# An attention gradient kernel: 32-row operands, steps in a fixed order, and some transposed probabilities from DMA instead of a second exponential

## The chip, the core and the metric

The kernel runs on one core of a Trainium2 chip. The metric is device time in microseconds (us) of one execution. TensorE multiplies matrices and writes to PSUM, ScalarE (ACT in the profile) does the exponentials, VectorE (DVE) and GpSimd (POOL) do element-wise work, and the DMA queues move and transpose data. Each kernel was timed in alternation with the kernel before on the same chip.

## The reference, cut to what matters

The reference is forward and backward of `out = x + attention(xn) * silu(mlp(xn))`, with 2048 positions, width 512, 32 heads of 16 channels, and gradients for x and all weights. The attention part is this; the change touches nothing else.

```python
scores = jnp.einsum("bhqd,bhkd->bhqk", q, k) * (Dh ** -0.5)   # 32 heads, 2048 x 2048
p = softmax(scores)
o = jnp.einsum("bhqk,bhkd->bhqd", p, v)                       # and, by jax.vjp, dq, dk, dv
```

## The kernel before

Two heads (a pair) are worked on together. The attention stage has 64 blocks (16 pairs times 4 groups of 512 queries) of 16 steps. In step g of a block (cut, names as in the kernel):

```python
# keys on partitions, 128 keys x 2 heads x 512 queries, for block j
s  = K^T Q        # TensorE     et = exp(s)     # ScalarE
d  = V^T dO       # TensorE     gts = d * et    # VectorE;  gk = transpose of gts by DMA
X += [V,K | 1 | ...] * et, gts   # TensorE: sums over keys, give o, row sums L and dq
# queries on partitions, for block j-1, whose row sums are known by now
t  = Q^T K        # TensorE     e = exp(t)      # ScalarE: the same probabilities a second time, transposed
Z += W1 * e + W2 * gk            # TensorE: sums over queries, give dk and dv; added to acc by VectorE
```

At the end of a block, X is copied (`xs`), transposed on TensorE (`XT`), copied (`xt`), and a chain of small operations on VectorE (`rL`, `dl`, `ndr`) and GpSimd makes `W1` and `W2` for the Z products. The parts that the change touches:

```python
ps_s = ... bufs=1        # s: one buffer, [128, 2, 512] fp32
ps_d = ... bufs=2        # t and d take turns in two buffers of the same size
def emit_r1(g):          # s(g), t(g), d(g), in this order
    ...
    for hj in range(2):
        r0 = 64 * hj     # each head takes 64 array rows; a pair fills all 128
        nc.tensor.matmul(s[:, hj, :], lhsT=op["KVT"][r0:r0 + 64, ...], rhs=op["QT"][r0:r0 + 64, ...], tile_position=(r0, 0))
    ...                  # t and d likewise
for g in range(...):     # the framework's scheduler may still move these
    emit_r1(g + 1)       # so d(g+1) is asked for before the multiply of step g
    emit_exp_a(g); emit_mult(g); emit_exp_b(g); emit_dmat(g)
    ...                  # X products of step g-1, Z products of step g-3
```

Of the kernel before, what the change touches and what calls it, by code (L numbers as in the profile page):

```python
# [8 lines left out]
bf16 = mybir.dt.bfloat16  # L9
# [533 lines left out]
NATW_CORE = 33  # L543
def attention_core(ctx, tc, NAT_s, NATQ_s, Oall, dQall, dKVT_out,
                   ident_f32, npairs=16, lagb=3, nqc=4, ekc=(), laga=1):
    nc = tc.nc
    S = 2048
    opnd = ctx.enter_context(tc.tile_pool(name="opnd", bufs=1))
    ps_s = ctx.enter_context(tc.tile_pool(name="ps_s", bufs=1, space=PSUM))
    ps_x = ctx.enter_context(tc.tile_pool(name="ps_x", bufs=1, space=PSUM))  # L550
    ps_z = ctx.enter_context(tc.tile_pool(name="ps_z", bufs=1, space=PSUM))
    ps_d = ctx.enter_context(tc.tile_pool(name="ps_dt", bufs=2, space=PSUM))
    ps_t = ps_d
    etp = ctx.enter_context(tc.tile_pool(name="etp", bufs=3 + laga))
    gtp = ctx.enter_context(tc.tile_pool(name="gtp", bufs=5))
    etsp = ctx.enter_context(tc.tile_pool(name="etsp", bufs=3)) if ekc else None
    gbp = ctx.enter_context(tc.tile_pool(name="gbp", bufs=6))
    ekp = ctx.enter_context(tc.tile_pool(name="ekp", bufs=2)) if ekc else None
    ep = ctx.enter_context(tc.tile_pool(name="ep", bufs=lagb + 2))
    xsp = ctx.enter_context(tc.tile_pool(name="xsp", bufs=1))  # L560
    finp = ctx.enter_context(tc.tile_pool(name="finp", bufs=2))
    wp = ctx.enter_context(tc.tile_pool(name="wp", bufs=2))
    accp = ctx.enter_context(tc.tile_pool(name="accp", bufs=1))
    outp = ctx.enter_context(tc.tile_pool(name="outp", bufs=1))

    OP = []
    for i in range(2):
        t = dict(
            KVT=opnd.tile([128, S], bf16, name=f"KVT{i}"),
            QT=opnd.tile([128, S], bf16, name=f"QT{i}"),  # L570
            DOT=opnd.tile([128, S], bf16, name=f"DOT{i}"),
            NAT=opnd.tile([128, 16, 2, NATW], bf16, name=f"NAT{i}"),
            NATQq=opnd.tile([128, 16, 2, 17], bf16, name=f"NATQq{i}"),
            NATQd=opnd.tile([128, 16, 2, 16], bf16, name=f"NATQd{i}"),
        )
        OP.append(t)
    KPad = opnd.tile([128, 16, 2, 64], bf16, name="KPad")
    QPad = opnd.tile([128, 16, 2, 64], bf16, name="QPad")
    DPad = opnd.tile([128, 16, 2, 64], bf16, name="DPad")
    nc.gpsimd.memset(KPad[:], 0.0)  # L580
    nc.gpsimd.memset(QPad[:], 0.0)
    nc.gpsimd.memset(DPad[:], 0.0)
# [3 lines left out]
    cur_op = {}  # L586
    load_q = []

    def load_pair(p, immediate=False):
        t = OP[p % 2]  # L590
        cur_op[p] = t
        eng = nc.sync
        ops = []

        def plain():
            eng.dma_start(out=t["NAT"][:].rearrange("q k j c -> q k (j c)"), in_=NAT_s[p])
            eng.dma_start(out=t["NATQq"][:].rearrange("q k j c -> q k (j c)"), in_=NATQ_s[0][p])
            eng.dma_start(out=t["NATQd"][:].rearrange("q k j c -> q k (j c)"), in_=NATQ_s[1][p])
        ops.append(plain)

        def tk():
            nc.gpsimd.tensor_copy(out=KPad[:, :, :, 0:NATW], in_=t["NAT"][:])
            eng.dma_start_transpose(out=t["KVT"][:].rearrange("r (m k) -> r m k", m=16), in_=KPad[:].rearrange("q k j c -> q (k j c)"))
        ops.append(tk)

        def tq():
            nc.gpsimd.tensor_copy(out=QPad[:, :, :, 0:17], in_=t["NATQq"][:])
            eng.dma_start_transpose(out=t["QT"][:].rearrange("r (m k) -> r m k", m=16), in_=QPad[:].rearrange("q k j c -> q (k j c)"))
        ops.append(tq)

        def td():
            nc.gpsimd.tensor_copy(out=DPad[:, :, :, 17:33], in_=t["NATQd"][:])
            eng.dma_start_transpose(out=t["DOT"][:].rearrange("r (m k) -> r m k", m=16), in_=DPad[:].rearrange("q k j c -> q (k j c)"))
        ops.append(td)
        if immediate:
            for o in ops:
                o()
        else:
            load_q.extend(ops)
# [4 lines left out]

    st_s = {}; st_d = {}; st_t = {}; st_et = {}; st_e = {}; st_gt = {}; st_ets = {}
    blk = [dict() for _ in range(NB + 1)]
    cur = dict(Z=None, gts=None)

    def a_unit(g):
        j = g // 16  # L630
        return (j, g % 16) if j < NB else None
# [4 lines left out]

    def emit_r1(g):
        a = a_unit(g); b = b_unit(g)
        if a is not None:
            j, kb = a  # L640
            p, qc = blocks[j]
            op = cur_op[p]
            s = ps_s.tile([128, 2, 512], f32, name="s")
            st_s[g] = s
            for hj in range(2):
                r0 = 64 * hj
                nc.tensor.matmul(s[:, hj, :], lhsT=op["KVT"][r0:r0 + 64, kb * 128:(kb + 1) * 128],  # L647
                                 rhs=op["QT"][r0:r0 + 64, qc * 512:(qc + 1) * 512],
                                 start=True, stop=True, tile_position=(r0, 0))
        if b is not None and b[1] not in ekc:  # L650
            j, kc, qb = b
            p, qc = blocks[j]
            op = cur_op[p]
            t = ps_t.tile([128, 2, 512], f32, name="t", tag="d")
            st_t[g] = t
            q0 = (qc * 4 + qb) * 128
            for hj in range(2):
                r0 = 64 * hj
                nc.tensor.matmul(t[:, hj, :], lhsT=op["QT"][r0:r0 + 64, q0:q0 + 128],  # L659
                                 rhs=op["KVT"][r0:r0 + 64, kc * 512:(kc + 1) * 512],  # L660
                                 start=True, stop=True, tile_position=(r0, 0))
        if a is not None:
            j, kb = a
            p, qc = blocks[j]
            op = cur_op[p]
            d = ps_d.tile([128, 2, 512], f32, name="d", tag="d")
            st_d[g] = d
            for hj in range(2):
                r0 = 64 * hj
                nc.tensor.matmul(d[:, hj, :], lhsT=op["KVT"][r0:r0 + 64, kb * 128:(kb + 1) * 128],  # L670
                                 rhs=op["DOT"][r0:r0 + 64, qc * 512:(qc + 1) * 512],
                                 start=True, stop=True, tile_position=(r0, 0))
        while fin_pending and fin_pending[0][1] <= g:
            emit_finalize(fin_pending.pop(0)[0])

    def emit_exp_a(g):
        a = a_unit(g)
        if a is None:
            return
        j, kb = a  # L680
        if (kb // 4) in ekc:
            if kb % 2 == 0:
                cur["ets"] = etsp.tile([128, 2, 2, 512], bf16, name="ets")
            ets = cur["ets"]
            st_ets[g] = ets
            et = ets[:, kb % 2]
        else:
            et = etp.tile([128, 2, 512], bf16, name="et")[:]
        st_et[g] = et
        nc.scalar.activation(out=et, in_=st_s.pop(g)[:], func=ACT.Exp)  # L690

    def emit_mult(g):
# [3 lines left out]
        j, kb = a  # L696
# [4 lines left out]
        nc.vector.tensor_tensor(out=gts[:, kb % 2], in0=st_d.pop(g)[:], in1=st_et[g], op=ALU.mult)  # L701

    def emit_dmat(g):
        a = a_unit(g)
        if a is None:
            return
        j, kb = a
        if kb % 2 == 1:
            kc = kb // 4
            kbp = (kb // 2) % 2  # L710
            if kbp == 0:
                blk[j].setdefault("Gk", {})[kc] = gbp.tile([128, 2, 16, 128], bf16, name="gk")
            gk = blk[j]["Gk"][kc]
            nc.sync.dma_start_transpose(out=gk[:, kbp], in_=st_gt[g][:].rearrange("k a h q -> k (a h q)"))
            if kc in ekc:
                if kbp == 0:
                    blk[j].setdefault("Ek", {})[kc] = ekp.tile([128, 2, 16, 128], bf16, name="ek")
                ek = blk[j]["Ek"][kc]
                nc.sync.dma_start_transpose(out=ek[:, kbp], in_=st_ets.pop(g)[:].rearrange("k a h q -> k (a h q)"))
                st_ets.pop(g - 1, None)  # L720

    def emit_exp_b(g):
        if b_unit(g) is None or b_unit(g)[1] in ekc:
            return
        e = ep.tile([128, 2, 512], bf16, name="e")
        st_e[g] = e
        nc.scalar.activation(out=e[:], in_=st_t.pop(g)[:], func=ACT.Exp)  # L727

    def emit_acc_a1(g):
        a = a_unit(g)  # L730
        if a is None:
            return
# [271 lines left out]
```

## Time and profile before

| | before |
|---|---|
| median time | 3006.6 us (3003.4 to 3009.0, 4 runs) |
| attention stage | 287 to 2393 us |
| median block | 32.66 us |
| exponentials per block | 32, one every 0.905 us at best: 29.0 us |

First the costliest groups on the page of the kernel before (line, engine, operation, out<-in, shapes, count | busy us, mean ns of one | idle time before them and what ended it).

```profile
L701 DVE TENSOR_TENSOR gts<-d,et 128x1024 bf16<-128x1024 f32 x1024 | 1251.5, 1222 | 555.9 <-ACT et L690 534.5
L690 ACT ACTIVATE et<-s 128x1024 bf16<-128x1024 f32 x1024 | 1050.5, 1026 | 161.5 <-PE s L647 126.7
L727 ACT ACTIVATE e<-t 128x1024 bf16<-128x1024 f32 x1024 | 1049.5, 1026 | 6.2 <-PE t L659 5.0
```

A mean of 1026 ns is not what an exponential costs. In the view of the instructions of the kernel before in time order, from which the next lines are taken (start us, duration us, engine, line, operation, [idle before <- what ended it]), one ScalarE instruction starts before the one ahead of it has ended.

```profile
1193.04 1.02 ACT L727 ACTIVATE e<-t 128x1024 bf16<-128x1024 f32 x1
...
1193.17 1.23 DVE L701 TENSOR_TENSOR gts<-d,et 128x1024 bf16<-128x1024 f32 x1 [0.84 <-ACT et L690]
...
1193.94 1.03 ACT L690 ACTIVATE et<-s 128x1024 bf16<-128x1024 f32 x1
1194.11 0.39 PE L659 MATMUL t<-KVT_2216,QT_2217 64*128 64x512 bf16 x2 [0.24 <-ACT e L727]
...
1194.45 0.39 PE L670 MATMUL d<-DOT_2218,KVT_2216 64*128 64x512 bf16 x2
...
1194.84 1.04 ACT L727 ACTIVATE e<-t 128x1024 bf16<-128x1024 f32 x1
...
1195.22 0.38 PE L829 MATMUL Z<-gk,W_14113 128*32 128x512 bf16 x2
...
1195.54 0.39 PE L647 MATMUL s<-QT_2217,KVT_2216 64*128 64x512 bf16 x2
...
1195.97 1.02 ACT L690 ACTIVATE et<-s 128x1024 bf16<-128x1024 f32 x1
```

From 1193.04 to 1193.94 and on to 1194.84 the starts are 0.90 us apart, with nothing idle. The Trainium skill, "ScalarE: Activation LUTs", "What ACT_TABLE_LOAD costs", says that back-to-back activations overlap by about 93 ns; here it is about 0.12 us. The next `et` starts only at 1195.97, 1.13 us after the `e` ahead of it, because its `s` (L647) started at 1195.54, at the end of a long row of products. So the steps alternate between about 1.83 and 2.03 us. Also note d (L670): at 1194.45 it starts 0.05 us after the multiply (L701, 1193.17 + 1.23) has ended. Of the eight steps between 1299 and 1316 us, six do the same, within 0.06 us; over the trace from 400 to 2150 us it is 87% of the d products. These start 0.34 us after their t, the others 0.22.

The view of busy time by stretch, for one stretch of 260 us of the kernel before, shows how full the engines are. Its columns are the stretch, its length, the busy us (and instructions) of PE, PE's weight loads, DVE, ACT and POOL, the granted TensorE clock, the DMA share and GB/s.

```profile
1000.00:1260.00 260.00, 234.14 (x2074) 68.94 (x2069) 192.83 (x208) 240.89 (x256) 29.03 (x78) 1.00 0.82 148
```

The view of the waits of the kernel before, between 400 and 2150 us (who <- for whom: us in total, times, longest), names who waits on ScalarE's path:

```profile
PE t L659 <- ACT e L727: 104.5, 394, 0.5
ACT et L690 <- PE s L647: 104.2, 152, 2.6
```

TensorE waits for `e` to give its buffer to t, and what stands behind t comes late, s among it, for which ScalarE then waits.

### The profile page before, as it was taken

What the parts mean: (1) busy time and instruction counts of PE and PEld (TensorE: products, weight loads), DVE (VectorE), ACT (ScalarE), POOL (GpSimd) and SP (SyncE); (2) the same over time, 40 slices, a digit from 0 to 9 for tenths busy, and PEclk for the clock granted to TensorE, in tenths of its full rate; (3) what the DMA queues carried; (4) which work ended last, traced back from release to release, by engine and by line L of the source; (5) the groups of instructions that cost most, each with busy time, mean ns of one, the idle gap of its engine ahead of it and who ended that gap; (6) DMA issues with size and microseconds to landing.
All of it is one profiled execution on the core that took longest, in us unless ns stands there. A gap on an engine that the chain in (4) does not pass through costs nothing. (4 is left out here: it accounts for less than half of the span.)

```text
span 2997.4 us, 50127 instructions
## 1 busy us (share of the span) xinstructions
PE 2491.3 (83%) x19909; PEld 859.6 (29%) x19968; DVE 2011.0 (67%) x2422; ACT 2205.8 (74%) x2485; POOL 583.2 (19%) x944
## 2 busy tenths in 40 slices
PE   3786998898899899899988988998898865665967
PEld 2332222222222222222222222222222233332443
DVE  5764777777777777777777777777777637882044
ACT  2442899998899999999999989999999824441020
POOL 0334011101101110110111011011101026881024
PEclk8898999999999999999999999999999987887989
DMA  5436888869878886987888698788867563325431
GB/s 169 120 127 145 142 151 138 162 130 157 142 147 149 142 162 132 160 145 148 153 138 161 132 158 142 148 153 137 162 132 130 107 230 94 103 81 153 127 127 41
DMA packets 1324301, 417.62 MB, mean 139 GB/s; under 512 B 1247393, under 2 KB 1308194, under 8 KB 1324066
## 3 DMA queue, kind: packets, MB, share of 16 engines
q1 hardware_dynamic: 1250674, 360.80, 63.0%
q10 hardware_dynamic: 73392, 53.62, 5.8%
q8 instruction: 156, 2.56, 0.3%
q14 instruction: 79, 0.65, 0.1%
HBM read 65.41 MB, written 55.32 MB: 40 GB/s over the span
## 5 line engine op out<-in xcount | busy, mean ns | idle before, releaser
L701 DVE TENSOR_TENSOR gts<-d,et 128x1024 bf16<-128x1024 f32 x1024 | 1251.5, 1222 | 555.9 <-ACT et L690 534.5
L690 ACT ACTIVATE et<-s 128x1024 bf16<-128x1024 f32 x1024 | 1050.5, 1026 | 161.5 <-PE s L647 126.7
L727 ACT ACTIVATE e<-t 128x1024 bf16<-128x1024 f32 x1024 | 1049.5, 1026 | 6.2 <-PE t L659 5.0
L742 PE MATMUL X<-et,Lc 128*32 128x512 bf16 x2048 | 403.2, 389 | 2.3 <-DVE xt L776 0.2
L659 PE MATMUL t<-KVT_2216,QT_2217 64*128 64x512 bf16 x1024 | 200.5, 380 | 63.8 <-ACT e L727 61.4
L659 PE MATMUL t<-KVT_2222,QT_2223 64*128 64x512 bf16 x1024 | 200.1, 380 | 64.0 <-ACT e L727 61.3
L647 PE MATMUL s<-QT_2217,KVT_2216 64*128 64x512 bf16 x1024 | 201.3, 388 | 15.2 <-DMA QT_2217<-QPad 15.1
L670 PE MATMUL d<-DOT_2218,KVT_2216 64*128 64x512 bf16 x1024 | 201.0, 381 | 11.8 <-DVE gts L701 6.2
L670 PE MATMUL d<-DOT_2224,KVT_2222 64*128 64x512 bf16 x1024 | 200.4, 380 | 4.8 <-DVE gts L701 2.8
L647 PE MATMUL s<-QT_2223,KVT_2222 64*128 64x512 bf16 x1024 | 199.9, 387 | 0.0
L758 PE MATMUL X<-gts,NAT_2219 128*17 128x512 bf16 x1024 | 198.0, 381 | 0.0
L758 PE MATMUL X<-gts,NAT_2225 128*17 128x512 bf16 x1024 | 197.4, 381 | 0.0
L745 PE MATMUL X<-et,NAT_2219 128*32 128x512 bf16 x1024 | 196.8, 391 | 0.0
L745 PE MATMUL X<-et,NAT_2225 128*32 128x512 bf16 x1024 | 196.4, 390 | 0.0
L742 PEld LDWEIGHTS <-Lc 128*32 128x32 bf16 x2048 | 100.4, 93 | 245.1 <-issue 236.8
L659 PEld LDWEIGHTS <-QT_2223 64*128 64x128 bf16 x1024 | 89.2, 94 | 188.7 <-issue 188.5
L659 PEld LDWEIGHTS <-QT_2217 64*128 64x128 bf16 x1024 | 89.2, 94 | 185.8 <-issue 185.6
L837 DVE TENSOR_TENSOR acc<-Z,acc 64x512 f32<-64x512 f32 x192 | 129.3, 673 | 8.7 <-PE Z L829 8.7
L670 PEld LDWEIGHTS <-KVT_2216 64*128 64x128 bf16 x1024 | 90.0, 93 | 138.4 <-issue 127.9
L670 PEld LDWEIGHTS <-KVT_2222 64*128 64x128 bf16 x1024 | 90.6, 93 | 126.4 <-issue 118.6
L647 PEld LDWEIGHTS <-KVT_2216 64*128 64x128 bf16 x1024 | 52.1, 93 | 224.9 <-issue 223.7
L647 PEld LDWEIGHTS <-KVT_2222 64*128 64x128 bf16 x1024 | 49.1, 93 | 218.0 <-issue 218.0
(1527 smaller groups left out, 3829.7 us busy)
## 6 DMA issues: line engine op xcount, KB each, us to landing
gk<-gts SPq DMA_TRANSPOSE x512, 4.3
HG_s<-hg SPq DMA_DIRECT2D x16, 448.0 KB, 2.9
GB_s<-gB ACTq DMA_DIRECT2D x16, 256.0 KB, 2.0
dKVT_s<-ob SPq DMA_DIRECT2D x16, 256.0 KB, 3.6
dhc<-DH_s ACTq DMA_DIRECT2D x2, 2048.0 KB, 13.6
H1T_s<-h1row SPq DMA_DIRECT2D x14, 256.0 KB, 2.0
H1T_s<-h1row ACTq DMA_DIRECT2D x14, 256.0 KB, 2.0
h1T<-H1T_s SPq DMA_DIRECT2D x8, 448.0 KB, 3.8
```

The source lines that it names most:

```text
L647: nc.tensor.matmul(s[:, hj, :], lhsT=op["KVT"][r0:r0 + 64, kb * 128:(kb + 1) * 128], rhs=op["QT"][r0:r0 + 64, qc * 512:(qc + 1) * 512], st ...
L659: nc.tensor.matmul(t[:, hj, :], lhsT=op["QT"][r0:r0 + 64, q0:q0 + 128], rhs=op["KVT"][r0:r0 + 64, kc * 512:(kc + 1) * 512], start=True, st ...
L670: nc.tensor.matmul(d[:, hj, :], lhsT=op["KVT"][r0:r0 + 64, kb * 128:(kb + 1) * 128], rhs=op["DOT"][r0:r0 + 64, qc * 512:(qc + 1) * 512], s ...
L690: nc.scalar.activation(out=et, in_=st_s.pop(g)[:], func=ACT.Exp)
L701: nc.vector.tensor_tensor(out=gts[:, kb % 2], in0=st_d.pop(g)[:], in1=st_et[g], op=ALU.mult)
L727: nc.scalar.activation(out=e[:], in_=st_t.pop(g)[:], func=ACT.Exp)
L742: nc.tensor.matmul(X[64 + 32 * hj:64 + 32 * hj + 32, :], lhsT=Lc[:, :], rhs=et[:, hj, :], start=(kb == 0), stop=False, skip_group_check=Tr ...
L745: nc.tensor.matmul(X[32 * hj:32 * hj + 32, :], lhsT=NATt[:, kb, hj, 1:33], rhs=et[:, hj, :], start=(kb == 0), stop=(kb == 15), tile_positi ...
L758: nc.tensor.matmul(X[64 + 32 * hj:64 + 32 * hj + 17, :], lhsT=NATt[:, kb, hj, 0:17], rhs=gts[:, kb % 2, hj, :], start=False, stop=(kb == 1 ...
L837: nc.vector.tensor_tensor(out=av, in0=Z[0:64, :], in1=av, op=ALU.add)
```

## The change

The intent: s, t and d take 32 rows each, so that d can run beside s; the steps are put in a fixed order by hand (`tc.manual_schedule()`), with s and t in turn in two buffers and d in two of its own; and 2 of the 16 `e` tiles of a block are not computed again but are DMA transposes (`ek`) of `et`. I call these two units the DMA part. The diff, cut to its core:

```diff
-    ps_s = ... (name="ps_s", bufs=1, space=PSUM)     # [128, 2, 512]
-    ps_d = ... (name="ps_dt", bufs=2, space=PSUM)    # [128, 2, 512], t and d
+    dma_units = ((1, 3), (3, 3))                     # (key group kc, query block qb) without a second exp
+    ps_st = ... (name="ps_st", bufs=2, space=PSUM)   # [128, 2, 512], s and t
+    ps_d = ... (name="ps_d", bufs=2, space=PSUM)     # [128, 512], one head of d each; XT too
 ... KVT, QT, DOT become KVT and QDT: 32 rows each for K0, K1, V0, V1 and q0, q1, dO0, dO1
+    def emit_t(g):
+        if b is None or b[1:] in dma_units:
+            return
 ...
+            r = 64 + 32 * hj
+            d = ps_d.tile([128, 512], f32, name="d", tag="d")
+            nc.tensor.matmul(d[:], lhsT=op["KVT"][r:r + 32, ...], rhs=op["QDT"][r:r + 32, ...], ..., tile_position=(r, 0))
 ...
-        nc.vector.tensor_tensor(out=gts[:, kb % 2], in0=st_d.pop(g)[:], in1=st_et[g], op=ALU.mult)
+        for hj in range(2):
+            nc.vector.tensor_tensor(out=gts[:, kb % 2, hj, :]..., in0=ds[hj][:]..., in1=st_et[g][:, :, kb % 4, hj, :], op=ALU.mult)
 ...
+                if (kc, qb) in dma_units:
+                    ek = ekp.tile([128, 8, 128], bf16, name="ek")
+                    nc.sync.dma_start_transpose(out=ek[:], in_=st_et[g][:, qb].rearrange("k a h q -> k (a h q)"))
 ...
+        emit_t(g)
+        if not first:
+            emit_le(g - 1)          # X products of et
+        emit_exp_b(g)
+        emit_s(g + 1)
+        emit_d(g)
+        emit_mult(g)
+        emit_exp_a(g + 1)
+        emit_dmat(g)
+        if first:
+            emit_le(g - 1)
+        emit_g(g - 1)               # X products of gts
+        emit_z(g - lagb, 0)         # Z products of e or ek
+        emit_z(g - lagb, 1)         # Z products of gk
+        if g >= 17 and (g - 17) % 16 == 0 and (g - 17) // 16 < NB:
+            emit_finalize((g - 17) // 16)
```

The small copies for `dKVT` go to GpSimd, and the operand transposes fall from three to two per pair.

## The prediction

> **What bounds it now.** The attention stage runs from 287 to about 2395 us, 70% of the span (instructions in time order): 64 blocks of 16 steps, about 32.5 us a block. A step has two 1024-wide exponentials on ScalarE, `et<-s` and `e<-t`. The groups give 1026 ns each, but in the time order one starts 0.905 us after the other when nothing holds it: ends overlap. So ScalarE's floor is 1.81 us a step, 29.0 us a block. Normal steps alternate between 1.83 and 2.05 us (mean 1.94): `s` has one PSUM buffer, and TensorE, in order, does s, t, d, X and Z products (about 1.5 us of slots of 0.22 to 0.34 us) with waits for `e` in between, so `s` comes late at times (`et <- PE s` in the waits: 113 us between 400 and 2300). The end of a block (XT transposes, W1, W2) costs about 1.5 us more. VectorE is busy 74% of the stage, DMA 82%; a 512 KB `gk` transpose streams for 2.5 us of every 4.
>
> **What changes.**
> 1. Two of 16 `e` exponentials per block become DMA transposes of `et`: 2 x 0.905 us off ScalarE, floor 27.2 us a block.
> 2. s, t, d take 32 rows each; d sits in other rows than s and follows it, so all four should run together. The Trainium skill, "TensorE: Matmul & The Clock Gate", Part 3, says that small matmuls in different row groups run concurrently. The trace agrees for pairs of 64 rows (one slot of 0.22 us); four of 32 no trace here shows yet. TensorE goes from six slots a step to five, about 1.4 us.
> 3. `s` and `t` alternate in two buffers: `s` can run during the preceding `e`, `t` during the preceding `et`, each with about 0.4 us to spare. ScalarE should be gapless in normal steps.
> 4. The multiply is split in two 512-wide ones with a one-bank d each. From the 512-wide copies (0.68 us, ends overlapping by 0.08) I estimate 0.6 us each, 1.2 us a step against 1.14. With acc, xs, xt and small ones VectorE needs 23.5 to 25 us a block, near ScalarE's floor but below.
> 5. DMA: per pair 32 `gk` as before, plus 8 half-size `ek`, minus one of three operand transposes; streaming about 12.5 of every 14.5 us. Close, not binding.
> 6. Steps without `e` can't quite keep 0.905 us: TensorE brings `t` about 0.2 us late. At the end of a block XT in the d buffers holds up d and t: I keep 1.0 us.
>
> **Sum.** 14 x 1.83 + 2 x 1.05 + 1.0 = 28.7 us a block against 32.5, nearly all on the critical path, as ScalarE paces the stage. 63 blocks x 3.8 = 240 us, a little more in the first. Other stages don't change. I predict 2760 us, range 2690 to 2850; faster by over 2%: 0.96, within 2%: 0.03, slower: 0.01.
>
> **What would show it.** `e<-t` 896 times, still 1.03 us; ScalarE starts 0.905 us apart in normal steps, busy over 95% of the stage's middle; `et <- PE s` well under 113 us; s and d starting together; `gts` 2048 times near 0.68 us; DMA share about 0.95; block period 28 to 29.5 us.
>
> **What would make it wrong.** Strided 256-byte runs slow the exponential or the multiply; VectorE (d single-buffered per half) becomes the pace; in-order TensorE waits for d and passes that to t; DMA queueing delays `gk`; four-row matmuls don't overlap.

## The result, and the profile after

| | before | after |
|---|---|---|
| median time | 3006.6 us | 2848.6 us (2847.5 to 2850.9, 4 runs) |
| ratio | | 0.948 (0.946 to 0.949) |
| median block | 32.66 us | 30.44 us |

Ratios here are the mean time of one kernel's runs over that of the other's of the same rounds, so not quite the ratio of the medians. The gain is 158 us; I had predicted 247. It lies in the attention stage, as foreseen: `et` starts there at 287 us in both, and the last `e` ends at 2392.9 us before and 2253.9 after.

The same groups on the page of the kernel after:

```profile
L697 DVE TENSOR_TENSOR gts<-d,et 128x512 bf16<-128x512 f32 x2048 | 1315.0, 683 | 374.6 <-ACT et L676 146.4
L676 ACT ACTIVATE et<-s 128x1024 bf16<-128x1024 f32 x1024 | 1058.1, 1056 | 11.8 <-PE d L662 11.7
L684 ACT ACTIVATE e<-t 128x1024 bf16<-128x1024 f32 x896 | 933.9, 1043 | 165.0 <-PE t L634 163.9
```

The multiply is 683 ns, as estimated, and `et` no longer waits for s. But `e<-t` waits 163.9 us for t, where before `e` had almost no idle time. The waits of the kernel after in the same window say it again:

```profile
ACT e L684 <- PE t L634: 144.1, 233, 1.0
...
PE s L648 <- ACT et L676: 108.6, 458, 0.5
```

Now s waits for ScalarE instead of ScalarE for s; t is the one that comes late.

In the same stretch of the kernel after, the DMA share is 0.98 (predicted 0.95), and VectorE is up from 193 to 208 us of 260.

```profile
1000.00:1260.00 260.00, 237.49 (x2188) 72.94 (x2180) 208.49 (x349) 238.90 (x258) 33.72 (x88) 1.00 0.98 171
```

Where the waits sit becomes plain from the time between the starts of consecutive `et`, taken from each trace, as a median per position in the block over blocks 4 to 59 (us; position 0 is from the block's first `et` to its second):

```
position       0    1    2    3    4    5    6    7    8    9   10   11   12   13   14   15
before      2.06 1.82 2.67 1.82 3.00 1.82 2.03 1.83 2.07 1.82 2.03 1.83 2.06 1.82 2.03 1.83
after       2.82 1.81 2.66 1.81 2.19 1.81 1.81 0.90 2.79 1.81 1.81 1.81 1.88 1.81 1.81 0.90
```

Normal steps after are 1.81 us, gapless, as predicted. Positions 7 and 15 are the steps without `e`: 0.90 us, one exponential saved. But the steps right behind them, 8 and 0, take 2.8 us, one microsecond too much. What was saved is given back one step later. This is one such place in the kernel after (instructions in time order):

```profile
1182.57 0.39 PE L648 MATMUL s<-QDT,KVT 32*128 32x512 bf16 x2
...
1182.58 0.39 PE L662 MATMUL d<-QDT,KVT 32*128 32x512 bf16 x2
...
1183.09 1.29 DVE L697 TENSOR_TENSOR gts<-d,et 128x512 bf16<-128x512 f32 x2 [0.60 <-ACT et L676]
...
1183.33 1.94 ACT L676 ACTIVATE et<-s 128x1024 bf16<-128x1024 f32 x2
...
1183.66 0.39 PE L648 MATMUL s<-QDT,KVT 32*128 32x512 bf16 x2
...
1183.84 0.37 PE L662 MATMUL d<-QDT,KVT 32*128 32x512 bf16 x1
1184.30 0.67 DVE L818 COPY acc<-Z 64x512 f32<-64x512 f32 x1
1184.43 0.37 PE L662 MATMUL d<-QDT,KVT 32*128 32x512 bf16 x1 [0.23 <-DVE gts L697]
...
1184.74 0.39 PE L744 MATMUL X<-gts,NAT 128*17 128x512 bf16 x2
...
1185.02 0.39 PE L807 MATMUL Z<-e,W 128*32 128x512 bf16 x2
...
1185.24 0.39 PE L813 MATMUL Z<-gk,W 128*32 128x512 bf16 x2
...
1185.57 0.39 PE L634 MATMUL t<-KVT,QDT 32*128 32x512 bf16 x2
...
1186.06 1.02 ACT L684 ACTIVATE e<-t 128x1024 bf16<-128x1024 f32 x1 [0.79 <-PE t L634]
```

At 1182.57 and 1182.58, s and d start together: the packing works as the Trainium skill, "TensorE: Matmul & The Clock Gate", Part 3, says of small matmuls in different row groups. At 1183.33 ScalarE does two `et` in a row (x2), for there is no t in this step. The next t (L634) could have started when the first of these was done, about 1184.3. But TensorE takes its work in order, and ahead of t stand the second half of d, which waits 0.23 us for the multiply that began at 1183.09; the X product of gts (0.31 us later); the Z product (0.28 us later, because `acc` (L818, started at 1184.30) still reads the one Z buffer); the second Z product (0.22 us); then t (0.33 us). So t starts at 1185.57 and `e` at 1186.06 after 0.79 us of idle time. The trace has the same sequence at all 112 steps of this kind in blocks 4 to 59: in the middle 80% of them t starts 2.28 to 2.31 us after the first of the two `et`. The prediction had said that t comes 0.2 us late. It had named d's wait, passed on to t, as a risk, but not put it into the sum.

### The profile page after: what moved, and what is told of

It is laid out like the page before. It is cut to its first block, busy times and chain, and to the rows that moved or that the text cites. A ratio compares the mean times of both kernels' runs of the same rounds, so it can differ in the third digit from the quotient of the medians.

```text
span 2849.1 us, 50869 instructions
## 1 busy us (share of the span) xinstructions
PE 2397.8 (84%) x19712; PEld 845.8 (30%) x19712; DVE 2029.7 (71%) x3382; ACT 2057.1 (72%) x2357; POOL 619.0 (22%) x1023
## 5 line engine op out<-in xcount | busy, mean ns | idle before, releaser
L697 DVE TENSOR_TENSOR gts<-d,et 128x512 bf16<-128x512 f32 x2048 | 1315.0, 683 | 374.6 <-ACT et L676 146.4
L684 ACT ACTIVATE e<-t 128x1024 bf16<-128x1024 f32 x896 | 933.9, 1043 | 165.0 <-PE t L634 163.9
L662 PE MATMUL d<-QDT,KVT 32*128 32x512 bf16 x2048 | 492.4, 382 | 30.5 <-DVE gts L697 28.5
L648 PE MATMUL s<-QDT,KVT 32*128 32x512 bf16 x2048 | 402.9, 385 | 135.7 <-ACT et L676 120.3
L732 PE MATMUL X<-et,NAT 128*32 128x512 bf16 x2048 | 405.5, 393 | 0.0
L744 PE MATMUL X<-gts,NAT 128*17 128x512 bf16 x2048 | 400.7, 388 | 0.0
L813 PE MATMUL Z<-gk,W 128*32 128x512 bf16 x2048 | 394.2, 379 | 0.0
L807 PE MATMUL Z<-e,W 128*32 128x512 bf16 x1792 | 351.3, 387 | 2.8 <-DVE acc L820 2.0
L634 PE MATMUL t<-KVT,QDT 32*128 32x512 bf16 x1792 | 349.9, 382 | 2.3 <-ACT e L684 2.3
L648 PEld LDWEIGHTS <-KVT 32*128 32x128 bf16 x2048 | 146.9, 91 | 399.3 <-issue 397.8
L634 PEld LDWEIGHTS <-QDT 32*128 32x128 bf16 x1792 | 103.9, 91 | 365.7 <-issue 365.7
L807 PEld LDWEIGHTS <-W 128*32 128x32 bf16 x2048 | 121.3, 93 | 55.3 <-issue 53.8
L662 PEld LDWEIGHTS <-KVT 32*128 32x128 bf16 x2048 | 108.1, 91 | 9.4 <-issue 1.0
L825 POOL CAST ob<-acc 64x512 bf16<-64x512 f32 x64 | 38.7, 605 | 313.3 <-DVE acc L820 311.3
L813 PEld LDWEIGHTS <-W 128*32 128x32 bf16 x2048 | 103.9, 96 | 7.5
```

Source lines behind the costliest of these rows:

```text
L634: nc.tensor.matmul(t[:, hj, :], lhsT=op["QDT"][r:r + 32, q0:q0 + 128], rhs=op["KVT"][r:r + 32, kc * 512:(kc + 1) * 512], start=True, stop= ...
L648: nc.tensor.matmul(s[:, hj, :], lhsT=op["KVT"][r:r + 32, kb * 128:(kb + 1) * 128], rhs=op["QDT"][r:r + 32, qc * 512:(qc + 1) * 512], start ...
L662: nc.tensor.matmul(d[:], lhsT=op["KVT"][r:r + 32, kb * 128:(kb + 1) * 128], rhs=op["QDT"][r:r + 32, qc * 512:(qc + 1) * 512], start=True, ...
L684: nc.scalar.activation(out=e[:], in_=st_t.pop(g)[:], func=ACT.Exp)
L697: nc.vector.tensor_tensor(out=gts[:, kb % 2, hj, :].rearrange("k (b q) -> k b q", b=4), in0=ds[hj][:].rearrange("k (b q) -> k b q", b=4), ...
L732: nc.tensor.matmul(X[32 * hj:32 * hj + 32, :], lhsT=NATt[:, kb, hj, 1:33], rhs=et[:, :, kb % 4, hj, :], start=(kb == 0), stop=(kb == 15), ...
```

## The experiments

My theory (A): the DMA part is worth nothing, because a step without `e` leaves ScalarE waiting for a late t; the 158 us come from the rest. Rivals: the DMA part gives the 0.7 us per step that I had predicted and the gain is missing elsewhere (B), or the added DMA load does the harm (C). A second question is what in the rest gave the 158 us. In all runs below, the medians of the kernel before in the same rounds lie between 3003.3 and 3008.3 us. Runs with values wrong keep every size; they say so.

### 1. Without the DMA part, and with its load alone

`no_dma` takes all 16 `e` per block. `spare_dma` does the same, but still issues the `ek` transposes for nobody.

```diff
-    dma_units = ((1, 3), (3, 3))
+    dma_units = ()
```
```diff
+                if (kc, qb) in ((1, 3), (3, 3)):      # spare_dma only: issued, never read
                     ek = ekp.tile([128, 8, 128], bf16, name="ek")
```

> Change without its DMA part: no unit from ek, all 16 second exponentials per block. Theory A (a step without e leaves ScalarE idle for about 0.95 us afterwards, because TensorE brings the next t too late, so the part is worth nothing): 2845 us, within 15 us of the change. Rival B (the prediction's account: each such step saves 0.7 us, and the missing gain was lost elsewhere): about 2940 us.

> As no_dma, but the ek transposes are still issued and nobody reads them. Theory A (order of TensorE, not DMA load): same as no_dma within 10 us. Rival C (the added DMA load itself holds up gk, gts or et and makes the idle time): slower than no_dma by 60 to 120 us.

Measured: `no_dma` 2849.5 us (ratio 0.948), `spare_dma` 2854.0 us (0.950), the change 2848.6 us. The DMA part moves the time by less than the spread of the runs. Rival B falls, and so does C: the load was there (DMA share 0.95 between 1000 and 1260 us, against 0.87 in `no_dma`), but without the use it costs about 4.5 us. In `no_dma`, positions 0, 7, 8 and 15 of a block take 1.91, 1.81, 1.88 and 1.81 us, together 7.4 us; in the change 2.82, 0.90, 2.79 and 0.90, also 7.4 us.

### 2. The late t

`t_early` puts the next t right behind d in a step without `e`. `q1` moves the DMA units away from the step behind `acc`. `t_early_q1` does both.

```diff
         emit_d(g)
+        if b_unit(g) is not None and b_unit(g)[1:] in dma_units:
+            emit_t(g + 1)          # and emit_t returns if g is already done
         emit_mult(g)
```
```diff
-    dma_units = ((1, 3), (3, 3))
+    dma_units = ((1, 1), (3, 1))
```

> The change, with one move: in the step without e, the t of the next step is put right behind d, ahead of the X and Z products. Theory A: idle time after such a step falls from about 1.0 to about 0.3 us, two per block, so 1.4 us a block: about 2765 us. Rival C (DMA load): no change, 2849 us.

> The change, with the two DMA units at (1,1) and (3,1) in place of (1,3) and (3,3), so that a step without e no longer comes right behind the sum into acc. If the wait of the Z product for acc (0.28 us in the trace) is a part of the late t, each idle time falls by about 0.3 us: about 2815 us. If only the wait of d for the multiply matters: 2849 us.

> The change with both moves: t put early in steps without e, and the DMA units away from acc. Theory A: idle after such a step falls from 1.0 us to 0.2 us or less, block 28.9 us, 2750 us (2735 to 2770). If something else than t and acc holds these steps: no better than 2802 us, the better of the two alone.

Measured: `t_early` 2801.7 us (0.933), `q1` 2810.0 us (0.936), `t_early_q1` 2757.0 us (0.918). All three are correct. `q1` came out as expected. `t_early` gave only half of what I expected: positions 0 and 1 became 2.05 and 2.27 us, so part of the idle time only moved one step on. In its trace, after such a step, `acc` runs ahead of the multiply and four halves of the multiply follow without a gap from 1206.15 to 1208.85; the second half of d, and the t after it, wait for them. With both moves the rest is gone too:

```
position       0    1    2    3    4    5    6    7    8    9   10   11   12   13   14   15
t_early_q1  1.94 1.81 2.65 1.81 2.19 0.90 1.81 1.94 1.94 1.81 1.81 1.81 1.88 0.90 1.81 1.97
```

The two steps without `e` (5 and 13) are 0.90 us, the steps right behind them 1.81, and little is paid back later (0.13 and 0.16 us more than in `no_dma` at positions 7 and 15): over the block 1.42 us of the 1.81 saved remain. One such step of `t_early_q1`, instructions in time order:

```profile
1212.08 1.96 ACT L677 ACTIVATE et<-s 128x1024 bf16<-128x1024 f32 x2
...
1213.20 0.37 PE L663 MATMUL d<-QDT,KVT 32*128 32x512 bf16 x1 [0.23 <-DVE gts L698]
...
1213.21 0.39 PE L635 MATMUL t<-KVT,QDT 32*128 32x512 bf16 x2
...
1213.89 1.07 ACT L685 ACTIVATE e<-t 128x1024 bf16<-128x1024 f32 x1
```

t (L635) starts beside the second half of d at 1213.21, and `e` starts at 1213.89 with no idle time noted, 1.81 us after the start of the two `et`. So what the DMA part is worth depends on TensorE's order: nothing as the change has it, 92 us (2849.5 less 2757.0) with t early and the units elsewhere. Theory A stands.

### 3. Packing and order

Here all runs build on `no_dma`. `same_rows` lets d read the rows of s, so that the two can't run side by side (values wrong). `old_order` goes back to s, t, d and then the X and Z products, but with d of step g, not g + 1. There d follows t, not s, and runs beside t: in its trace it starts 0.01 us after t. `old_same` is both (values wrong).

```diff
-            r = 64 + 32 * hj       # same_rows, old_same: in emit_d
+            r = 32 * hj
```
```diff
-        emit_t(g)                  # old_order, old_same
-        if not first:
-            emit_le(g - 1)
         emit_exp_b(g)
         emit_s(g + 1)
+        emit_t(g + 1)
         emit_d(g)
+        if not first:
+            emit_le(g - 1)
```

> no_dma (2849 us), with the packing of d beside s undone: d reads the same 32-row groups as s, so it must follow s instead of running beside it. Values wrong on purpose, sizes the same. Theory D (the new order has about 0.3 us to spare in a normal step, so the sixth slot costs only at the end of a block and after acc): 2880 to 2900 us. Rival E (packing is what freed ScalarE): normal steps grow by 0.2 us, 3000 us and more.

> no_dma with TensorE's order as before the change (s, t, d, then the X and Z products), packing kept. Theory D': with five slots the old order just fits behind e: 2850 to 2900 us. Rival F (the order by hand is what freed ScalarE): every s comes about 0.2 us late again, 3000 us and more.

> no_dma with the old order and without the packing; values wrong on purpose. Theory D and D' (either of the two is enough for normal steps): normal steps grow to about 1.95 us, 2970 to 3010 us, near the kernel before. If the two are simply additive or neither matters: near the sum of the two runs above.

| median us | d in rows of its own, packed | d in the rows of s and t, not packed |
|---|---|---|
| order by hand | 2849.5 | 2908.5 |
| old order | 2846.1 | 2883.4 |

Rivals E and F fall: `same_rows` lies 8 us above the range of theory D and `old_order` 4 us below that of D', but most steps stay at 1.81 to 1.83 us. TensorE's order by hand in the normal steps is worth nothing when d is packed, and it is the worse of the two when d is not. My expectation for `old_same` was wrong: its normal steps are 1.86 us, not 1.95. The packing is worth 37 us in the old order, 8 of them in the first two blocks. In the order by hand it shows 59 us (one of the four runs of `same_rows` took 2941.8 us; the median is used), but some 20 of these are at the start, where the second block took 47.7 us against 33.6 in `no_dma`: its granted clock was 0.50 from 287 to 370 us (more on this in section 5); later blocks take 31.10 us against 30.51. So neither explains the bulk of the gain: `old_same` has neither and is still 122 us faster than the kernel before in the same rounds.

### 4. The small operations at the end of a block

Position 4 takes 3.00 us before and 2.19 after. In the kernel before, the scheduler had put the last part of W1 behind the other small operations (its instructions in time order; L825 is the Z product):

```profile
1204.61 0.20 DVE L785 RECIPROCAL rL<-xt 128x8 f32<-128x8 f32 x1
...
1206.56 0.16 DVE L790 SCALAR_TENSOR_TENSOR ndr<-dl,rL 128x8 f32<-128x8 f32 x1
...
1207.33 0.40 POOL L801 TENSOR_TENSOR dQall<-t_14566,rL_14569 128x128 bf16<-128x128 f32 x1
...
1207.84 0.40 POOL L792 TENSOR_TENSOR W_14553<-NATQq_2220,ndr 128x128 bf16<-128x128 bf16 x1
...
1208.29 0.39 PE L825 MATMUL Z<-e,W_14553 128*32 128x512 bf16 x2 [0.88 <-POOL W_14553 L792]
```

`ndr` (L790) came 1.95 us after `rL` (L785), and W1 (L792) came after `dQall` (L801), which nobody waits for. TensorE stood still for 0.88 us. The run `late_w` puts that one operation last again in `no_dma`.

```diff
-        nc.gpsimd.tensor_tensor(out=W1[:, :, :, 16:32], in0=nqs, in1=bc(ndr[:]), op=ALU.mult)
 ...
         nc.gpsimd.tensor_tensor(out=dQv, in0=t1[:], in1=bc(rL4[:]), op=ALU.mult)
+        nc.gpsimd.tensor_tensor(out=W1[:, :, :, 16:32], in0=nqs, in1=bc(ndr[:]), op=ALU.mult)
```

> no_dma (2849 us) with one part of W1 computed last of GpSimd's small operations at the end of a block, as the scheduler had placed it in the kernel before (where the Z product waited 0.88 us for it). Theory G (the order by hand of these small operations is worth about 0.9 us a block of the gain): W1 comes about 1.7 us later, step 3 to 5 of a block grows by 0.5 to 1.0 us, 2880 to 2915 us. If the new lag or slack hides it: 2849 us.

Measured: 2910.8 us (0.969), 61 us slower than `no_dma`. Position 4 is 3.03 us, as in the kernel before, and the waits of `late_w` between 400 and 2150 us have TensorE waiting for that operation (L788 here):

```profile
PE Z L807 <- POOL W L788: 39.9, 55, 0.8
```

Theory G stands: some 61 of the 158 us come from the place of one 0.4 us operation on an engine that is busy 13% of the time there (33.73 of 260 us in `no_dma`).

### 5. Rows and buffers

`old_same` is faster than before by 122 us, and 61 of these are now known, if the parts add. What remains is mostly the normal steps (positions 5 to 15), 1.93 us before and 1.86 in `old_same`. `rows64` gives s, t and d 64 rows again (values wrong).

```diff
-            r = 32 * hj            # in s, t and d, on old_same
+            r = 64 * hj
-            ... [r:r + 32, ...]
+            ... [r:r + 64, ...]
```

> old_same (2883 us) with operands of 64 rows instead of 32 for s, t and d, as before the change; values wrong on purpose. Theory H (pairs that fill all 128 rows can't load their next weights early: in the trace of before d started 0.34 us after t, in old_same 0.22 us): normal steps grow from 1.86 to about 1.93 us, 2940 to 2960 us. Rival I (the separate PSUM buffers of d, not the rows, made the difference): 2883 us, steps as in old_same.

Measured: 2871.4 us (0.955), and every position of the block within 0.02 us of `old_same`. Theory H falls: the number of rows does not set the steps. That `rows64` is even 12 us faster comes from the start, where the first two blocks take 24.1 and 30.6 us against 30.3 and 36.9. The view of busy time by stretch shows it for the start of the stage, here of `old_same` (the granted clock is the third number from the right):

```profile
287.00:310.00 23.00, 20.86 (x100) 2.95 (x100) 12.89 (x20) 12.59 (x13) 0.00 (x0) 0.50 0.48 92
310.00:330.00 20.00, 20.00 (x104) 3.99 (x104) 13.53 (x23) 12.62 (x13) 1.80 (x5) 0.50 0.77 155
330.00:350.00 20.00, 19.14 (x138) 4.30 (x136) 11.62 (x19) 16.13 (x17) 3.61 (x9) 0.68 0.56 90
```

and of `rows64`:

```profile
287.00:310.00 23.00, 22.14 (x146) 3.88 (x143) 18.85 (x30) 15.08 (x16) 0.00 (x0) 0.86 0.79 143
310.00:330.00 20.00, 17.50 (x157) 4.72 (x158) 15.44 (x27) 19.24 (x22) 5.40 (x13) 1.00 0.92 168
```

With 32 rows the clock stays at 0.50 for over 40 us, though PE is shown busy for 20.0 of 20 us; with 64 rows it is 1.00 from 310 us on. The kernels with right values differ in the same way: in the stretch from 287 to 310 us the clock is 0.93 in the kernel before (64 rows), and 0.50 in the change and in `no_dma` (32 rows).

`old_bufs` then puts the PSUM buffers of before into `old_same`: one for s, t and d in turn in two, d a step early, one 1024-wide multiply (values wrong).

```diff
-    ps_st = ... bufs=2             # s and t
+    ps_st = ... bufs=1             # s alone; t and d share ps_d, [128, 2, 512] x 2
 ...
         emit_t(g + 1)
-        emit_d(g)
-        ...
         emit_mult(g)
+        emit_d(g + 1)
```

> old_same (2883 us) with the PSUM buffers and the place of d as before the change: one buffer for s, t and d taking turns in two, d computed one step early and multiplied in one 1024-wide operation; values wrong on purpose. Theory J (in the kernel before, d reuses the buffer of the previous d and so waits for the multiply of that step, each step, ahead of the X and Z products and the next s): d starts at the end of the multiply, 0.33 us after t instead of 0.22, normal steps grow from 1.86 to 1.93 us, 2930 to 2970 us. Rival K (neither buffers nor the early d): 2883 us, steps as in old_same.

Measured: 3871.3 us (1.286), which neither theory expected. A stretch of its mid-stage, in the same view:

```profile
1000.00:1500.00 500.00, 423.81 (x2776) 98.58 (x2774) 253.30 (x265) 329.47 (x343) 44.88 (x114) 0.66 0.56 101
```

The granted clock is 0.66 here and between 0.61 and 0.71 in every other stretch of the stage after 400 us, and products take 0.6 us for long times. This run says nothing clean about buffers, because the clock moved with them. So the last part of the gain is not settled by an experiment: that before, d waits for the multiply in its buffer ahead of all later products, is read from the traces, not shown by a run. Between 400 and 2150 us, 87% of the d products start within 0.06 us of the multiply's end in the kernel before, 9% in `old_same`. The single buffer of s, which the prediction blamed, looks less likely: only 6% of the s products before start within 0.08 us of the end of the `et` that frees it. Other differences between the two kernels were not undone one by one: XT in the buffers of d, the small copies on GpSimd, the multiply in two halves, one operand transpose less. So d's wait is the likeliest reading, and it stays open.

### 6. A try at a better kernel

`t_early_q1` already beats both kernels. `spread` tries to lessen the remaining cost at the end of a block as well (positions 2 and 4: 0.84 and 0.38 us above 1.81).

```diff
-    dma_units = ((1, 3), (3, 3))
-    lagb = 3
+    dma_units = ((1, 3), (2, 3))
+    lagb = 6
 ... t early as in run 2, gbp 7 buffers
-        if g >= 17 and (g - 17) % 16 == 0 and (g - 17) // 16 < NB:
-            emit_finalize((g - 17) // 16)
+        if g >= 18 and (g - 18) % 16 == 0 and (g - 18) // 16 < NB:
+            emit_finalize((g - 18) // 16)
```

> A try at a better kernel: t put early in steps without e, DMA units at (1,3) and (2,3), the Z products six steps behind instead of three, XT one step later, so that xs, acc, XT and the steps without e fall on different steps. If the end of a block costs 1.2 us because these pile up: block about 28.2 us, about 2705 us (2685 to 2740). If it costs that wherever XT stands: 2757 us, as t_early_q1.

Measured: 2749.7 us (0.914), correct, the fastest of all, but 45 us short of what I expected. Position 4 is now 1.81 us, but 2 and 3 take 2.10 and 2.51: most of the cost moved along with XT, though which of the moves did what was not tested. The steps without `e` take 1.14 us instead of 0.90. From 1000 to 1260 us both `t_early_q1` and `spread` show a DMA share of 1.02; their waits for engines name no DMA yet, but I would not expect room for more transposes (not tested).

## Why the prediction was right or wrong

The measured 2848.6 us lies inside the range, but 1.4 us from its end and 89 us from the expected 2760. That it lies inside is luck: the transposes in place of `e`, which the sum counts at about 100 us, gave nothing, and much of the gain came for reasons that the prediction did not have.

- **ScalarE paces the stage, 0.905 us apart, normal steps gapless at 1.81 us.** Right: the table of positions shows 1.81. That ScalarE would be busy over 95% of the middle was wrong: 238.9 of 260 us, 92%, and before it was 93%.
- **"Steps without `e` can't quite keep 0.905 us: TensorE brings `t` about 0.2 us late."** This is the term that was wrong. Each one lost about 1.0 us. What stood ahead of t in the trace is d's wait for the multiply (0.23 us idle), the X product (0.31 us after d), the Z product behind `acc` (0.28 us), and two more slots of 0.22 and 0.33 us. By the prediction's own numbers the DMA part should have given 16 x 1.83 + 1.0 less 28.7, that is 1.58 us a block or about 100 us; it gave nothing (2849.5 against 2848.6). That is more than the missing 89 us; the rest of the change gave a little more than the sum had for it. The mechanism, a late t, was right and only its size was wrong, for 92 us come back when t is put first and the units are moved.
- **End of a block, 1.0 us.** Nearly right: positions 2 and 4 cost 1.23 us. But I took its old cost for 1.5 us without seeing that 0.9 of it was one badly placed operation; before, the same two positions cost 2.05 us over 1.81. That XT in the buffers of d is what costs is not shown: position 2 takes 2.67 us before too, where XT sits in the buffer of X.
- **The rest of the gain.** The size was right (I had 32.5 to 30.3 us a block without the DMA part; `no_dma` has 30.5), the reasons mostly were not. I gave the credit to the packing and to s and t in turn. The packing is worth 37 us (59 in the order by hand) and the order of TensorE's products none; 61 us are the small operations, and most of the rest (158 - 61 - 37 = 60 us, if the parts simply add) is what I read as d's wait for the multiply, which stays open.
- **Multiply 0.6 us each, groups near 0.68; s and d together; DMA share 0.95; 896 `e`.** Right: 683 ns, starts 0.01 us apart, 0.97 to 0.99 in the middle of the stage, 896.
- **Block 28 to 29.5 us, 28.7 expected.** Wrong: 30.44.
- **First block.** I expected a little more gain there. It got slower, 27.9 us against 25.6, with the clock at 0.50.

## What to carry to other kernels

Here, work taken off the pacing engine was gained only where the engine that feeds it could deliver earlier in that very place (nothing against 92 us): look at what stands ahead of the feeding product in its engine's order, and move it to the front when you take work away. Before crediting a large rewrite to its main idea, undo its parts one by one; here one small operation on a nearly idle engine was worth as much as the array packing or more (61 us against 37 and 59). When a step waits, check whether it begins right when some other operation ends: 0.05 us after it, time and again, is more likely a wait than a gap of the engine.

## What the Trainium skill lacked or had wrong

- "TensorE: Matmul & The Clock Gate", Part 1, says that the granted clock follows how busy TensorE has recently been, and that warm-up takes about 3.4 us of sustained work. Here it also followed the number of rows: with pairs of 64 rows (`rows64`) it was 0.86 in the first 23 us of the stage and then 1.00, with pairs of 32 rows in the same kernel (`old_same`) 0.50 for over 40 us, at 20.0 of 20 us shown busy. In `old_bufs`, with 32 rows and the old buffers, it stayed at 0.61 to 0.71 from 400 us to the end of the stage (3871 us). Part 3 recommends 32-row tiles without a word on this.
- "ScalarE: Activation LUTs", "What ACT_TABLE_LOAD costs", has back-to-back activations overlap by about 93 ns; here it was about 120 ns (1.02 to 1.03 us long, 0.90 to 0.905 us apart).
- "DMA: Bandwidth & Descriptors", "Latency and other measured facts", gives 261 GB/s for DMA transposes with a non-contiguous middle dimension and 350 to 400 for contiguous ones. The `gk` transposes of 512 KB from SBUF to SBUF ran slower: the DMA view of one of them before the change (1163.1 to 1165.6 us) shows 0.50 MB at a mean of 199 GB/s.
